# Summing the first hidden product of a feed-forward layer during the attention before it

## The chip, the cores and the metric

The kernel runs on one NeuronCore of a Trainium2 chip. Its five engines work through queues of their own and wait for each other by semaphores: TensorE (PE in the profile, its weight loads PEld), VectorE (DVE), ScalarE (ACT), GpSimd (POOL) and SyncE (SP), which issues the DMAs here. The metric is the device time of one execution in microseconds. The three runs of the kernel before took 629.36, 629.53 and 629.88 us.

## The reference

Attention over q, k, v of 2 batches, 8 heads, 768 positions and 64 columns per head; a key is kept if it is one of the first 8 or lies less than 96 positions back. Then two feed-forward layers over the 1536 tokens, 512 wide with 2048 hidden columns.

```
scores = q k^T / 8 + bias(distance, head), others -1e9;  a = softmax(scores);  x = a v
h = x @ w_in ;  g = h * tanh(log1p(exp(h)))                           # first layer ("mish")
x = g @ w_out
h = x @ w_in2;  g = h if h>=1, 0 if h<=-1, else (h+1)^2/4             # second layer
out = g @ w_out2
```

## The kernel before, in words

All instructions stand in an order written out by hand; each engine works through its own in that order. The kernel has one stretch for the attention and one for the two layers.

**Attention.** A unit s is a batch, a pair of heads and two blocks of 128 queries (u = 0, 1): 24 units, three per pair, eight pairs. The loop at the end of `attention_windows` goes through rounds s = -1 to 27, and each round works on several units at once: `scores(s+1)` (line 327, TensorE), `transposes(s-2)` (364), `values(s-3)` (382), `softmax(s, u)` (339 on VectorE, 344 on ScalarE), `normalise(s-1)` (349 and 350 on VectorE, 354 on GpSimd), and `evict(s-2, u)` (170 on ScalarE, 172 on VectorE), which copies the transposed weights out of PSUM. A finished pair of output columns is rounded into `x_hi` by ScalarE (170), and VectorE subtracts to get `x_lo` (175). Every later product is made of three: high by high, high by low, low by high.

**PSUM.** Eight banks. Before, the scores of even units lie in banks 0 and 1, those of odd units in 6 and 7 (`SC`), the transposes in 2 and 3, the values in 4 and 5. Both halves u of a unit share a bank for each of the two heads j. The scores of a block against 256 keys are two instructions per head, which the profile counts singly: eight per unit.

**Weights.** Each layer has 16 blocks f of 1 MB, which SP loads, and which three engines turn into a high and a low part: `T` (scale, line 162 or 166), `B` (229, ScalarE), `V` (233 and 236, VectorE), `H` (round, 170) and `R` (subtract, 175), each for the two halves i of a block. The first three blocks (`PRE`) are converted during the attention, at the end of the rounds that `BESIDE` names; `T20` is the `T` of block 2, half 0. `FIRST_ON` says on which engine `T`, `H` and `R` run: `p` GpSimd, `a` ScalarE, `v` VectorE.

**Feed-forward.** A step n is a layer, a batch and a block f: `hidden(n)` (lines 519, 520 and 522: 12 products of 512 columns and 12 of 256), `gate(n)` (528 to 559, ScalarE and VectorE), and `finish`, the output products of the step before (570). The first steps are begun beside the attention: `h0a`, `h0b` are the 512 and the 256 columns of `hidden(0)`, `h1a`, `h1b` those of `hidden(1)`, and `g0a` to `g0c` the three parts of `gate(0)`. `out_T(0)`, in `finish`, also uses banks 0 to 5, so it follows the last `x_lo` out of banks 4 and 5.

```
    24: ("h0a",), 25: ("h0b", "g0a"), 26: ("g0b", "h1a", "g0c"), 27: ("h1b",),
```

Of the kernel before, what the change touches and what calls it, by code (L numbers as in the profile page):

```python
# [20 lines left out]
P = 128  # L21
# [9 lines left out]
FIRST_ON = "ppaapp"  # L31
# [14 lines left out]
def attention_then_two_ffn_kernel(  # L46
# [141 lines left out]
    class Weights:  # L188
# [15 lines left out]
        def convert(self, pool, m, f):  # L204
# [12 lines left out]
            on = FIRST_ON if first else LATER_ON  # L217
# [66 lines left out]
    SC, TR, PV, HID = ((0, 1), (6, 7)), (2, 3), (4, 5), (6, 7)  # L284

    def attention_windows(x_hi, x_lo, bank, wts, opening):
        with ExitStack() as es:
# [29 lines left out]
            scs, probs, pts = {}, {}, {}  # L317
            done = []

            def scores(s):  # L320
                b, p, t = steps[s]
                qr, kr = raws[b, p]
                scs[s] = [bank(SC[s % 2][j], [2, 2 * P]) for j in range(2)]
                for u in range(2):
                    i = 2 * t + u
                    for j, ps in enumerate(scs[s]):
                        nc.tensor.matmul(ps[:, u, 0:keys(i)], qr[half(j), i * P:(i + 1) * P],  # L327
                                         kr[half(j), window(i):window(i) + keys(i)], start=True, stop=True)

            def softmax(s, u):  # L330
# [6 lines left out]
                for j, ps in enumerate(scs[s]):  # L337
# [18 lines left out]

            def transposes(s):
                pr = probs.pop(s)[0]
                pts[s] = (pp.tile([P, 2, 2, 2, P], F32, tag="pts", name=f"pts{s}"),
                          [bank(TR[u], [2, 2, P]) for u in range(2)])  # L360
                for u, pt in enumerate(pts[s][1]):
                    for j in range(2):
                        for o in range(keys(2 * steps[s][2] + u) // P):
                            nc.tensor.transpose(pt[:, j, o], pr[:, u, j, o * P:(o + 1) * P], ident)  # L364

            def evict(s, u):
                m = keys(2 * steps[s][2] + u) // P
                dst, src = pts[s]
                rounded("av"[u], dst[:, u, :, 0:m], src[u][:, :, 0:m])

            def values(s):
                b, p, t = steps[s]
                vr = vs[b, p]
                src = pts.pop(s)[0]
                for u in range(2):
# [4 lines left out]
                    for o in range(m):  # L380
                        for j in range(2):
                            nc.tensor.matmul(pv[half(j), i * P - t0:(i + 1) * P - t0], vr[:, 2 * i - m + 1 + o, j],  # L382
                                             src[:, u, j, o], start=(o == 0), stop=(o == m - 1))
# [5 lines left out]
            for s in range(-1, NU + 4):  # L389
# [34 lines left out]
    def attention_all(x_hi, x_lo, bank, wts, opening):  # L424
        with ExitStack() as es:
# [31 lines left out]
            for b in range(B):  # L457
                for p in range(NP):
# [6 lines left out]
                    for j in range(2):  # L465
                        h = 2 * p + j
                        ro = slice(j * D, (j + 1) * D)
                        for pv, (t0, n) in zip(pvs, pieces):
                            for i in range(t0 // P, (t0 + n) // P):
                                ps = [bank(c, [n]) for c, (t, n) in zip(SC[rows % 2], pieces)]  # L470
# [31 lines left out]
            for name in sum((BESIDE[s] for s in sorted(BESIDE)), ()):  # L502
                if name[0] != "b":
                    opening[name]()
                    if name in ("V11", "V21"):
# [3 lines left out]
    class FeedForward:  # L509
        def __init__(self, x_hi, x_lo, bank, xy, gp, tp, wts):  # L510

            def hidden(m, f, t, banks):
                xh, xl = (x[:, :, t * span[m]:(t + 1) * span[m]] for x in (x_hi, x_lo))
                wh, wl = (t[:, 0].rearrange("p (c f) -> p c f", f=P) for t in wts.parts[m, f])
                for (t0, n), u in zip(parts[m], banks):
# [7 lines left out]
                    yield ph  # L523

# [98 lines left out]
            def hidden_of(n):  # L623
                if n < len(steps):
                    m, b, f = steps[n]
                    phs[n] = list(hidden(m, f, b, (HID, HID[n % 2:])[m]))

            def hidden_piece(n):
                if n not in phs:
                    phs[n] = []  # L630
                    m, b, f = steps[n]
                    gens[n] = hidden(m, f, b, SC[n])
# [18 lines left out]
            self.hidden_piece, self.gate_part = hidden_piece, gate_part  # L651
# [103 lines left out]
```

## Time and profile before

| | |
|---|---|
| median of three runs | 629.53 us |
| the profiled execution | 626.96 us |
| its span, first to last instruction | 625.1 us |
| busy: PE, PEld, DVE, ACT, POOL | 608.3, 508.8, 420.4, 389.6, 59.3 us |
| mean granted TensorE clock | 0.999 |

A profile holds one execution. Its time is 1.9 us above its span, since start and end of the program lie outside it, and 2.6 us below the median of the other runs. Busy times are sums over the span. In a timeline each line has the start in us, the duration in us, the engine, the line of the code and the operation, output and inputs, shapes, how many were merged (x8), and in brackets how long the engine was idle ahead of it and who released it. The chain of waits goes back from the last instruction to what released each, and so tells which work set the end.

### The profile page before, as it was taken

The page shows a single profiled execution, that of the slowest core. Times are in us where ns is not written, and L with a number is a line of the kernel's source. Part 1 is how long each engine was busy: PE and PEld are TensorE (multiplying, and loading weights), DVE is VectorE, ACT ScalarE, POOL GpSimd, SP SyncE. Part 2 cuts the span into 40 slices and gives each one's busy share as a digit, 9 for nine tenths or more (in the row PEclk, how much of TensorE's full clock was granted, in tenths as well). Part 3 has the DMA queues.
Part 4 walks back from the last instruction along what each step waited for, and adds up shares of the span by engine and source line. Part 5 has one row for each costly group of instructions (what it writes and reads, how often), then busy time and mean ns, then how long its engine had stood idle before and what let it go on. Part 6 is the DMA issues. An engine that isn't in the chain of part 4 may idle for free.

```text
span 625.1 us, 9403 instructions
## 1 busy us (share of the span) xinstructions
PE 608.3 (97%) x3408; PEld 508.8 (81%) x3408; DVE 420.4 (67%) x970; ACT 389.6 (62%) x845; POOL 59.3 (9%) x122
## 2 busy tenths in 40 slices
PE   5999999999999999999999999999999999999996
PEld 3677678888888888888888888888888888888884
DVE  7899959999999777797877876664333333433332
ACT  5999957888888566686776777574433333433332
POOL 3787630000000000000000000000000000000000
PEclk9999999999999999999999999999999999999999
DMA  7995302443333102221312312300100000100002
GB/s 203 328 310 184 114 2 69 134 135 109 104 127 136 68 0 69 69 78 59 135 68 68 135 68 75 127 2 1 67 1 1 1 0 1 67 1 1 1 0 73
DMA packets 10421, 49.83 MB, mean 80 GB/s; under 512 B 1408, under 2 KB 1664, under 8 KB 6272
## 3 DMA queue, kind: packets, MB, share of 16 engines
q1 hardware_dynamic: 10368, 49.16, 23.7%
q8 instruction: 29, 0.48, 0.3%
q14 instruction: 24, 0.20, 0.1%
HBM read 46.01 MB, written 3.15 MB: 79 GB/s over the span
## 4 chain that ended last, share of the span: by engine, by line
PE 88%; DVE 8%; ACT 1%; SPq 1%; DMA 0%; issue 0%; POOL 0%; DVEq 0%; ACTq 0%
PE psum L570 22%; PE psum L579 21%; PE psum L519 14%; PE psum L520 14%; PE psum L522 14%; DVE pr L339 3%; PE psum L327 1%; DVE pts L172 1%; PE psum L364 1%; PE psum L382 1%; DVE st L349 1%; DVE wbits L236 1%; DVE x_lo L175 1%; ACT pr L344 1%; DMA qr<-in_q_dram 0%
## 5 line engine op out<-in xcount | busy, mean ns | idle before, releaser
L519 PE MATMUL psum<-x_hi,whi 128*128 128x512 f32 x448 | 157.0, 360 | 0.0
L520 PE MATMUL psum<-x_lo,whi 128*128 128x512 f32 x448 | 157.0, 360 | 0.0
L522 PE MATMUL psum<-x_hi,wlo 128*128 128x512 f32 x448 | 106.1, 359 | 0.0
L519 PEld LDWEIGHTS psum<-x_hi,whi 128*128 128x128 f32 x448 | 84.3, 188 | 14.7 <-issue 0.5
L520 PEld LDWEIGHTS psum<-x_lo,whi 128*128 128x128 f32 x448 | 84.5, 189 | 12.8
L522 PEld LDWEIGHTS psum<-x_hi,wlo 128*128 128x128 f32 x448 | 77.7, 189 | 12.5
L559 DVE TENSOR_TENSOR g_lo<-e,g_hi 128x512 fp32r<-128x512 f32 x112 | 65.9, 612 | 32.6 <-ACT g_hi L557 32.6
L543 ACT ACTIVATE e<-psum 128x512 f32<-128x512 f32 x48 | 28.7, 598 | 88.2 <-PE psum L522 88.2
L557 ACT ACTIVATE g_hi<-e 128x512 fp32r<-128x512 f32 x112 | 59.6, 560 | 36.8 <-DVE e L548 31.8
L544 DVE TENSOR_SCALAR e<-e 128x512 f32<-128x512 f32 x48 | 20.5, 427 | 82.9 <-ACT e L543 82.9
L579 PE MATMUL psum<-whi,g_hi 128*128 128x512 f32 x192 | 74.8, 390 | 0.5 <-ACT g_hi L557 0.5
L579 PE MATMUL psum<-whi,g_lo 128*128 128x512 f32 x192 | 74.8, 390 | 0.0
L579 PE MATMUL psum<-wlo,g_hi 128*128 128x512 f32 x192 | 74.7, 389 | 0.0
L570 PE MATMUL psum<-g_lo,whi 128*128 128x512 f32 (+1 forms) x256 | 67.3, 344 | 0.0
L570 PE MATMUL psum<-g_hi,wlo 128*128 128x512 f32 (+1 forms) x256 | 65.7, 338 | 0.0
L570 PE MATMUL psum<-g_hi,whi 128*128 128x512 f32 (+1 forms) x256 | 65.7, 338 | 0.0
L528 ACT ACTIVATE e<-psum 128x512 f32<-128x512 f32 x64 | 31.3, 491 | 52.1 <-PE psum L522 51.7
L548 DVE TENSOR_TENSOR e<-psum,e 128x512 f32<-128x512 f32 x48 | 33.2, 692 | 31.2 <-ACT e L545 31.2
L344 ACT ACTIVATE pr<-pr,st 128x256 f32<-128x256 f32 (+1 forms) x96 | 46.0, 481 | 11.0 <-DVE st L339 9.4
L236 DVE SCALAR_TENSOR_TENSOR wbits<-wsc,wbits 128x512 uint32<-128x512 uint32 x58 | 40.1, 692 | 12.8 <-ACT wbits L229 9.4
L229 ACT ACTIVATE wbits<-stage 128x512 uint16<-128x512 uint16 x62 | 48.3, 778 | 0.0
L354 POOL TENSOR_SCALAR pr<-pr,st 128x256 f32<-128x256 f32 (+1 forms) x96 | 44.2, 482 | 22.8 <-DVE st L350 9.6
(67 smaller groups left out, 898.6 us busy)
## 6 DMA issues: line engine op xcount, KB each, us to landing
stage<-in_w_dram SPq DMA_DIRECT2D x31, 1024.0 KB, 4.9
vr<-in_v_dram SPq DMA_DIRECT2D x8, 704.0 KB, 8.4
out_dram<-stage SPq DMA_DIRECT2D x12, 256.0 KB, 2.3
kr<-in_k_dram SPq DMA_DIRECT2D x14, 216.0 KB, 9.5
qr<-in_q_dram SPq DMA_DIRECT2D x7, 384.0 KB, 9.7
third<-in_w_dram SPq DMA_DIRECT2D x1, 1024.0 KB, 12.3
kr<-in_k_dram SPq DMA_DIRECT2D x2, 144.0 KB, 2.8
qr<-in_q_dram SPq DMA_DIRECT2D x1, 256.0 KB, 3.0
```

What stands on the lines that cost most here:

```text
L229: nc.scalar.activation(bits[:, i, :, 0], words(U16, i, 1), AF.Copy, scale=2.0 ** -13, bias=2.0 ** -14 - 0.5)
L236: nc.vector.scalar_tensor_tensor(out[:, i].bitcast(U32), moved(i, U32), 3, out[:, i].bitcast(U32), op0=ALU.logical_shift_left, op1=ALU.bit ...
L344: nc.scalar.activation(pr[:, u, j, 0:n], pr[:, u, j, 0:n], AF.Exp, scale=-1.0, bias=st[:, u, j, 0:1], accum_out=st[:, u, j, 1:2])
L354: nc.gpsimd.tensor_scalar(pr[:, u, j, 0:n], pr[:, u, j, 0:n], st[:, u, j, 3:4], 1.0, op0=ALU.mult, op1=ALU.mult)
L519: nc.tensor.matmul(ph, wh[:, c], xh[:, c, tok], start=(c == 0), stop=False)
L520: nc.tensor.matmul(ph, wh[:, c], xl[:, c, tok], start=False, stop=False)
L522: nc.tensor.matmul(ph, wl[:, c], xh[:, c, tok], start=False, stop=(c == KD - 1))
L548: nc.vector.tensor_tensor(e, ph, e, op=ALU.max)
L557: nc.scalar.activation(hi[:, t0:t0 + n], e, AF.Copy)
L559: nc.vector.tensor_tensor(lo[:, t0:t0 + n], e, hi[:, t0:t0 + n].bitcast(F32), op=ALU.subtract)
L570: nc.tensor.matmul(y, lhs[:, w], rhs[:, t0:t0 + n], start=(f == 0 and i == 0 and c % share == 0), stop=(f == NF - 1 and i == 2 and c % sha ...
L579: nc.tensor.matmul(ys[c], lhs[:, w], rhs, start=(f == 0 and i == 0), stop=(f == NF - 1 and i == 2))
```

## The change

The scores get two banks, 6 and 7, for all units, and are issued in two parts: the half u = 0 of the next unit behind `softmax(s, 0)`, the half u = 1 behind `softmax(s, 1)`. The banks 0 and 1 that this frees hold `hidden(0)`, which is summed during rounds 10 to 17: `h0a0` is the 512 columns for the first pair's 128 rows of x, `h0b3` the 256 columns for the fourth pair's. A transpose of 128 by 128 becomes two of 64 rows each, into banks 2 and 3, and `evict(s, c)` copies the half c of all of a unit's blocks. `values` moves behind the second part of the scores. Weight block 2 is converted at the end of the attention, its two subtractions on VectorE instead of GpSimd, and the load of block 4 is issued at round 13 instead of 19.

```diff
-FIRST_ON = "ppaapp"
+FIRST_ON = ("ppaapp", "ppaapp", "ppaavv")
-    8: ("V01", "H00"), 9: ("H01", "R00"), 11: ("R01", "T10", "B10"), 12: ("T11", "V10", "B11"),
-    13: ("V11", "H10"), 14: ("R10", "H11"), 16: ("R11",), 17: ("T20", "B20"), 18: ("T21", "V20", "B21"),
-    19: ("V21", "H20"), 20: ("R20", "H21"), 22: ("R21",),
-    24: ("h0a",), 25: ("h0b", "g0a"), 26: ("g0b", "h1a", "g0c"), 27: ("h1b",),
+    8: ("V01", "H00"), 9: ("H01", "R00"), 10: ("h0a0",), 11: ("R01", "T10", "B10", "h0a1"),
+    12: ("T11", "V10", "B11", "h0b0"), 13: ("V11", "H10", "h0b1"), 14: ("R10", "H11", "h0a2"), 15: ("h0b2",),
+    16: ("R11", "h0a3"), 17: ("h0b3",), 19: ("T20",), 20: ("T21",),
+    23: ("g0a",), 24: ("g0b", "h1a", "B20"), 25: ("g0c", "V20", "B21", "h1b"), 26: ("V21", "H20", "H21", "R20", "R21"),
...
-    SC, TR, PV, HID = ((0, 1), (6, 7)), (2, 3), (4, 5), (6, 7)
+    SC, TR, PV, HID = (6, 7), (2, 3), (4, 5), ((0, 1), (6, 7))
...
+            scs = [bank(c, [2, 2 * P]) for c in SC]
...
-            def scores(s):
+            def scores(s, u):
...
+                for n, (u, j, o) in enumerate(blocks(s)):
+                    for c, pt in enumerate(pts[s][1]):
+                        nc.tensor.transpose(pt[:, n], pr[half(c), u, j, o * P:(o + 1) * P], ident[half(c), half(c)])
...
+            def evict(s, c):
+                n = len(blocks(s))
                 dst, src = pts[s]
+                rounded("av"[c], dst[:, 0:n, half(c)], src[c][:, 0:n])
...
+                if 0 <= s < NU:
+                    softmax(s, 0)
                 if s + 1 < NU:
-                    scores(s + 1)
+                    scores(s + 1, 0)
                 if 0 <= s - 2 < NU:
                     transposes(s - 2)
-                if 0 <= s - 3 < NU:
-                    values(s - 3)
-                if 0 <= s < NU:
-                    softmax(s, 0)
                 if 0 <= s - 1 < NU:
                     normalise(s - 1)
...
                 if 0 <= s < NU:
                     softmax(s, 1)
+                if s + 1 < NU:
+                    scores(s + 1, 1)
+                if 0 <= s - 3 < NU:
+                    values(s - 3)
                 if 0 <= s - 2 < NU:
                     evict(s - 2, 1)
                 for name in BESIDE.get(s, ()):
                     opening[name]()
-                    if name in ("V11", "V21"):
+                    if name == "V11":
+                        wts.load()
                         wts.load()
...
+            def hidden_slice(c, t0, n):
+                wh, wl = (t[:, 0].rearrange("p (c f) -> p c f", f=P) for t in wts.parts[0, 0])
+                ph = bank(HID[0][0 if t0 == 0 else 1], [n])
+                tok = slice(t0, t0 + n)
+                for i, (w, x) in enumerate(((wh, x_hi), (wh, x_lo), (wl, x_hi))):
+                    nc.tensor.matmul(ph, w[:, c], x[:, c, tok], start=(c == 0 and i == 0),
+                                     stop=(c == KD - 1 and i == 2))
```

## Rows read from the trace of the kernel before

**Rows 1.** Windows by stage: stretch, length, busy PE, PEld, DVE, ACT, POOL (instructions), clock, DMA, GB/s.
```profile
64.00:82.00 18.00, 16.19 (x160) 12.22 (x159) 17.68 (x67) 16.09 (x55) 13.04 (x26) 1.00 0.20 84
82.00:100.40 18.40, 17.99 (x130) 14.90 (x131) 11.54 (x28) 9.46 (x24) 2.67 (x6) 1.00 0.00 1
100.40:356.00 255.60, 255.60 (x1455) 223.41 (x1454) 219.96 (x447) 193.67 (x387) 0.00 (x0) 1.00 0.27 91
```

**Rows 2.** Chain of waits in rounds 3 to 5: start, us, engine, output, line, merged.
```profile
15.50 0.81 PE psum L382 x12
16.30 1.06 PE psum L327 x8
...
18.39 1.02 PE psum L382 x16
19.41 0.86 PE psum L327 x8
```

**Rows 3.** Timeline of DVE: where softmax(s, 1) begins, for several rounds s.
```profile
31.15 0.41 DVE L339 CUSTOM_DVE_ANT_0 pr<-psum,bias 128x256 f32<-128x256 f32 x1
...
37.87 0.40 DVE L339 CUSTOM_DVE_ANT_0 pr<-psum,bias 128x256 f32<-128x256 f32 x1
...
43.94 0.41 DVE L339 CUSTOM_DVE_ANT_0 pr<-psum,bias 128x256 f32<-128x256 f32 x1
...
51.68 0.41 DVE L339 CUSTOM_DVE_ANT_0 pr<-psum,bias 128x256 f32<-128x256 f32 x1
...
57.20 0.39 DVE L339 CUSTOM_DVE_ANT_0 pr<-psum,bias 128x256 f32<-128x256 f32 x1
...
61.09 0.41 DVE L339 CUSTOM_DVE_ANT_0 pr<-psum,bias 128x256 f32<-128x256 f32 x1
...
71.89 0.41 DVE L339 CUSTOM_DVE_ANT_0 pr<-psum,bias 128x256 f32<-128x256 f32 x1
...
75.14 0.41 DVE L339 CUSTOM_DVE_ANT_0 pr<-psum,bias 128x256 f32<-128x256 f32 x1
...
77.40 0.39 DVE L339 CUSTOM_DVE_ANT_0 pr<-psum,bias 128x256 f32<-128x256 f32 x1
...
81.30 0.41 DVE L339 CUSTOM_DVE_ANT_0 pr<-psum,bias 128x256 f32<-128x256 f32 x1
```

**Rows 4.** Timeline of PE: the scores of unit 19 and of unit 22.
```profile
64.80 1.13 PE L327 MATMUL psum<-kr,qr 64*128 64x256 f32 x8
...
72.37 1.47 PE L327 MATMUL psum<-kr,qr 64*128 64x256 f32 x8 [0.98 <-DVE st L339]
```

**Rows 5.** Chain of waits at h0a and h0b: the last four products of each.
```profile
86.29 0.92 PE psum L522 x4
...
90.24 0.47 PE psum L522 x4
```

**Rows 6.** Timeline of POOL: the first scaling of weight block 0.
```profile
24.45 0.67 POOL L166 TENSOR_SCALAR stage<-stage 128x512 f32<-128x512 f32 x1 [2.33 <-DMA stage<-in_w_dram]
```

**Rows 7.** Timeline of DVE: the copy in round 7, V00, a slow L349, a subtraction of weights.
```profile
27.47 0.69 DVE L172 COPY pts<-psum 128x512 f32<-128x512 f32 x1 [0.91 <-PE psum L364]
...
28.43 0.45 DVE L233 TENSOR_SCALAR wbits<-stage 128x512 uint16<-128x512 uint16 x1
28.98 0.69 DVE L236 SCALAR_TENSOR_TENSOR wbits<-stage,wbits 128x512 uint32<-128x512 uint32 x1
...
53.39 1.11 DVE L349 TENSOR_SCALAR st<-st 128x4 f32<-128x4 f32 x1
...
104.23 0.68 DVE L175 TENSOR_TENSOR wlo<-wbits,whi 128x512 fp32r<-128x512 f32 x1
```

**Rows 8.** Timeline: the first exponential of gate(0), and the first weight load of hidden(2).
```profile
88.22 0.59 ACT L528 ACTIVATE e<-psum 128x512 f32<-128x512 f32 x1
...
100.37 0.19 PEld L519 LDWEIGHTS psum<-x_hi,whi 128*128 128x128 f32 x1
```

**Rows 9.** DMA issues of weight blocks: count, size of one, median us from issue to landing.
```profile
stage<-in_w_dram SPq DMA_DIRECT2D x31, 1024.0 KB, 4.9
```

More of the change, by code (lines that the diff above doesn't have):

```diff
@@ L216, in convert @@
             bits = out.rearrange("p a (n two) -> p a n two", two=2)
-            on = FIRST_ON if first else LATER_ON
+            on = FIRST_ON[f] if first else LATER_ON
             def moved(i, dtype):
@@ L316, in attention_windows @@
             NU = len(steps)
-            scs, probs, pts = {}, {}, {}
+            scs = [bank(c, [2, 2 * P]) for c in SC]
+            probs, pts = {}, {}
             done = []
-            def scores(s):
+            def scores(s, u):
                 b, p, t = steps[s]
                 qr, kr = raws[b, p]
[L323 to L328, printed above, removed]
+                i = 2 * t + u
+                for j, ps in enumerate(scs):
+                    nc.tensor.matmul(ps[:, u, 0:keys(i)], qr[half(j), i * P:(i + 1) * P],
+                                     kr[half(j), window(i):window(i) + keys(i)], start=True, stop=True)
             def softmax(s, u):
@@ L336, in softmax @@
                 n = keys(2 * t + u)
-                for j, ps in enumerate(scs[s]):
+                for j, ps in enumerate(scs):
                     h = 2 * p + j
@@ L355, in normalise, with blocks @@
                                                 op0=ALU.mult, op1=ALU.mult)
+            def blocks(s):
+                t = steps[s][2]
+                return [(u, j, o) for u in range(2) for j in range(2) for o in range(keys(2 * t + u) // P)]
             def transposes(s):
                 pr = probs.pop(s)[0]
[L359 to L367, printed above, removed]
+                pts[s] = (pp.tile([P, 8, P], F32, tag="pts", name=f"pts{s}"), [bank(TR[c], [8, D]) for c in range(2)])
+                for n, (u, j, o) in enumerate(blocks(s)):
[3 more added lines that the diff above has]
+                n = len(blocks(s))
                 dst, src = pts[s]
-                rounded("av"[u], dst[:, u, :, 0:m], src[u][:, :, 0:m])
+                rounded("av"[c], dst[:, 0:n, half(c)], src[c][:, 0:n])
             def values(s):
@@ L374, in values @@
                 src = pts.pop(s)[0]
+                place = {x: n for n, x in enumerate(blocks(s))}
                 for u in range(2):
@@ L382, in values @@
                             nc.tensor.matmul(pv[half(j), i * P - t0:(i + 1) * P - t0], vr[:, 2 * i - m + 1 + o, j],
-                                             src[:, u, j, o], start=(o == 0), stop=(o == m - 1))
+                                             src[:, place[u, j, o]], start=(o == 0), stop=(o == m - 1))
                     if (i + 1) * P == t0 + n:
@@ L469, in attention_all @@
                             for i in range(t0 // P, (t0 + n) // P):
-                                ps = [bank(c, [n]) for c, (t, n) in zip(SC[rows % 2], pieces)]
+                                ps = [bank(c, [n]) for c, (t, n) in zip(HID[rows % 2], pieces)]
                                 rows += 1
@@ L504, in attention_all @@
                     opening[name]()
-                    if name in ("V11", "V21"):
+                    if name == "V11":
+                        wts.load()
                         wts.load()
@@ L625, in hidden_of @@
                     m, b, f = steps[n]
-                    phs[n] = list(hidden(m, f, b, (HID, HID[n % 2:])[m]))
+                    phs[n] = list(hidden(m, f, b, (HID[1], HID[1][n % 2:])[m]))
             def hidden_piece(n):
@@ L631, in hidden_piece @@
                     m, b, f = steps[n]
-                    gens[n] = hidden(m, f, b, SC[n])
+                    gens[n] = hidden(m, f, b, HID[1])
                 phs[n].append(next(gens[n]))
@@ L680, in arm @@
                 opening.update(wts.convert(wpa, 0, f)[0])
-            opening.update({f"h{n}{i}": lambda n=n: ff.hidden_piece(n) for n in range(2) for i in "ab"})
+            opening.update({f"h1{i}": lambda: ff.hidden_piece(1) for i in "ab"})
+            opening.update({f"h0{i}{c}": lambda c=c, t=t: ff.hidden_slice(c, *t) for i, t in zip("ab", pieces)
+                            for c in range(KD)})
             opening.update({f"g0{i}": lambda: ff.gate_part(0) for i in "abc"})
```

4 lines of the change are left out of this document (3 added, 1 removed).

## The prediction, made before the changed kernel was run

> **What bounds the kernel now.** I read the busy times first, then the windows by stage, the chain of waits in order of time, and the timelines of single engines where the chain changes hands. The windows [rows 1] show three stages. From 100.4 us on TensorE is busy without a gap, and nothing in the change touches that stretch: it moves as a block. So the question is only when hidden(2), the first product of that block, can start; before, its first weight load stands at 100.37 us [rows 8]. Up to 82 us VectorE is busy 17.68 of 18.00 us [rows 1]: the reader is to see that the attention's second part is bound by VectorE, not by TensorE. Its first part, up to 31 us, is bound by TensorE: in the chain [rows 2] scores take 1.06 us, the transposes behind them some 1.02, values 1.02, and the next scores follow at once. In the tail, 82 to 100.4 us, VectorE has 11.54 us of work in 18.40 and TensorE 17.99 [rows 1].
>
> I split the time at E, the end of the last read of scores. softmax(23, 1) begins at 81.30 us [rows 3]; its second head follows 0.34 us later and takes some 0.42, so E = 82.06, and from E to hidden(2) there are 18.3 us.
>
> **The change part by part: the loop through one pair of banks.** Which bank a product waits for is seen at 72.37 us [rows 4]: the scores of unit 22 stood 0.98 us until softmax(20, 1), begun at 71.89 [rows 3], had read its first head, although their first half goes into columns that softmax(20, 0) had freed two microseconds earlier. So waits go by the bank, not by its half. With one pair of banks this gives a chain: softmax(s, 1), scores(s+1, 1), then on TensorE's queue values(s-3) and any slice of hidden(0), then scores(s+2, 0), and softmax(s+1, 1) must wait for these since they write its bank. Each term from rows: 0.48 us from the start of the softmax to the scores (71.89 to 72.37); 0.34 for the second head's bank (1.47 against 1.13 us of a group that needn't wait [rows 4]); half a group of scores to the next group, 1.06 less 0.43, which is 0.63 (0.43 is twice 0.21, the difference of 16 and 12 value products of the same columns [rows 2]); values 1.02 [rows 2]; a half group to its result, 1.13 less 0.43, 0.70. Sum 3.17 us a round; 2.96 where values has 12 products and 2.97 where scores(s+2, 0) has 128 columns, so 9.10 per pair of heads. A round without weight work took VectorE 2.26 us (75.14 to 77.40 [rows 3]): the wait is new, and some 0.9 us of it stand idle on VectorE. Queued behind the waiting softmax are the copy of the transposes and all weight work of that round, and ScalarE's exponentials wait for it.
>
> **The slices.** The last four products of h0a take 0.92 us, of h0b 0.47 [rows 5]: 0.23 and 0.12 each. Three, with 0.2 for the change of shape on TensorE (0.63 less 0.43, above), make 0.89 for h0a and 0.55 for h0b, all of it in the loop, ahead of scores(s+2, 0).
>
> **Transposes.** The eight transposes of a unit took 1.02 us, 0.82 without the change of shape [rows 2]. The trace has none on half the rows. From below two halves run side by side at half the columns, 0.41 us. From above I go by the nearest row: a unit whose first block has 128 keys takes 0.86 us for its scores, 0.20 less than others [rows 2], so four loads of 64 rows by 128 columns with their products take 0.43 less 0.20, 0.23 us, and sixteen 0.92. Both ends cost nothing here: they begin 0.27 us ahead of softmax(s, 1) (0.70 less 0.43), so end at the latest 0.65 after it, while the second head's scores cannot begin before 0.82. The copies keep their 512 columns, and each now waits for the whole unit; VectorE reaches its copy 0.68 us after the softmax, so this too is covered.
>
> **Rounds 8 to 22.** Each takes the longer of the loop and VectorE's own work. 8 and 9 stay at VectorE's 6.72 (31.15 to 37.87); 10 is 2.97 + 0.89 = 3.86; 11 and 14 are 4.06 each; 12 and 13 stay at VectorE's 7.74 (43.94 to 51.68), above the loop's 7.03; 15 is 3.51; 16 stays at 3.89 (57.20 to 61.09); 17 is 3.72. Rounds 18 to 21 lose V20, V21 and one slow L349: that line took 1.11 us [rows 7] where a subtraction of weights ran on GpSimd. VectorE would need about 2.4 a round there, so the loop's 2.96, 2.97, 3.17 and 2.96 hold, 12.06 together. Round 22 had 3.90 with such a stall (77.40 to 81.30) and keeps 2.26 with a remainder of 0.68, about 3.0. Sum 52.62 us against 50.15 before (31.15 to 81.30 [rows 3]): 2.5 us longer. In rounds 3 to 7 the loop's 9.10 stands against 8.7 per pair of heads (scores, transposes and values of two full units and one with twelve products [rows 2]), about 1.1 us later by round 7; but there VectorE waited 0.91 us for transposes [rows 7] that stood behind GpSimd's scaling, and this behind the landing of a weight block at 24.45 us [rows 6]. That moment doesn't move, so the lag is taken up: +0.1, at most +1.4. E comes 2.6 us later, at 84.7.
>
> **The tail.** Out of it go h0a and h0b, 4.6 us of TensorE (twelve products at 0.23 and 0.12, and two changes of shape). Into VectorE's share come V20 and V21, 0.45 + 0.69 each, and R20 and R21, 0.68 each [rows 7]: 3.6 us. VectorE had 11.54 us there [rows 1], of which about 1.0 lies behind what hidden(2) needs (the 512 columns of step 1 read from bank 6). 11.54 + 3.6 - 1.0 = 14.2. Two waits come to it: the first exponential of gate(0), 0.59 us [rows 8], stands behind two of the last softmax and ends 0.7 us after VectorE is free; and about 0.2 at each of four hand-overs from ScalarE, an estimate. That makes 15.7 us from E to hidden(2) where there were 18.3: the tail returns 2.6 of the 4.6. The last x_lo stands behind V21, R20 and R21 on VectorE's queue, and out_T(0) needs its bank; that is where the rest goes. From below stands TensorE's own work: some 0.8 until unit 22's transposes can begin, two groups of transposes at 1.02, values 0.81 and twice 1.02 [rows 2], hidden(1) 4.6 like hidden(0), and the 24 products of out_T(0), of the same two widths, 4.2, which makes 14.5; from above, another 1 us of hand-overs makes 16.7.
>
> **The load.** Block 4 is issued behind block 3 at the end of round 13, shortly before 51.68 us [rows 3], and the last q and k stand behind it on SP's queue. They are read by the scores that round 20 issues, near 70 us (softmax(20, 1) begins at 71.89 [rows 3]). A load of this size lands in 4.9 us [rows 9], and from 64 us on the DMA engines are busy 0.20 of the time [rows 1]; coming 5 us later costs nothing. If that cover were gone, round 20 would slip by as much.
>
> **Sum.** +2.5 + 0.1 - 2.6 = 0.0 us. The profiled execution's span of 625.1 and its 626.96 stay; the median of the runs lies 2.57 above that, so 629.5 us. The range of this case by itself is 627.5 to 631.5.
>
> **A rule against it.** Four half loads and their products took 0.23 us in the scores, as worked out above [rows 2]. The Trainium skill ("TensorE: Matmul & The Clock Gate", LDWEIGHTS) says that a load's time goes by its columns, not its rows, about 107 ns for 128. By that, and with loads one after another, 16 half loads would take 1.71 us and the kernel, as an estimate, about 639. The scores' rows speak against it, as two loads there share such a time.
>
> **The rivals.**
> *The loop is shorter.* The terms of 0.34 and 0.70 come from whole groups; with both banks free together and half a group's result at 0.6 the loop is 0.48 + 0.63 + 1.02 + 0.6, 2.73. Nine rounds (10, 11, 14, 15, 17 and 18 to 21) win 0.44 each, 4.0 us: 625.5. For it: groups that needn't wait show no 0.34. Against: the two heads of a softmax are always 0.34 apart.
> *No wait by the bank.* If the product needn't wait for the bank's other half, the sums of VectorE and TensorE bind. TensorE has two half groups of 0.43, transposes near 0.6, values 1.02 and two changes of shape, 2.9 in a full round at most and 2.5 in a lean one; with a slice 3.4 or 3.1. Rounds 8, 9, 12, 13 and 16 keep 18.35, rounds 10, 11 and 14 take 10.2, 15 and 17 6.2, 18 to 21 10.2 and 22 3.0: 47.95, 2.2 less than before, and with the tail 624.7. The wait at 72.37 speaks against it.
> *Slower: ScalarE closes the loop.* Its copy of bank 2 waits for the whole unit's transposes, and ahead of the next L349 stand this copy (0.5) and two exponentials (1.0). Ending 0.6 after the softmax, with 0.3 to be seen, the transposes let L349 begin at 2.4 us and, with the reciprocal and a remainder, the next softmax at 3.4: 0.2 beyond the loop. It decides as soon as the copy ends later than 1.1 us after the softmax. At 0.2 us on 15 rounds it costs 3 us: 632.5. For it: ScalarE is busy 16.09 of 18.00 us in the attention's second part [rows 1]. Against: two rounds of three have no long remainder.
> *A half costs as much as a whole.* Then sixteen transposes take twice 0.82, 1.64 us, and end 0.55 past the moment at which the second head's scores could begin: nine rounds in full, others in part, some 8.5 us: 638. Against it: the 0.23 us of the scores.
>
> **Chances.** The forecast 0.42; the shorter loop 0.22; no wait by the bank 0.10; ScalarE 0.22; halves as dear as wholes 0.04. 0.2%, or 1.26 us, is about what a measurement of this kernel can tell from no change. The forecast's own spread gives faster 0.10, same 0.26, slower 0.06; the shorter loop faster 0.19, same 0.03; the third all faster; ScalarE slower 0.18, same 0.04; the last slower. Together faster 0.39, same 0.33, slower 0.28. The range runs from 624.6 to 633.0.
>
> **What would show it.** Right: VectorE's line 339 waits for line 327 by some 0.9 us in rounds 18 to 21, which take 2.9 to 3.2; rounds 10, 11, 14 about 4; the last softmax read near 84.7 us; hidden(2) near 100.4, with VectorE waited for ahead of out_T(0)'s bank 5 and TensorE idle there. Wrong: 327 never waited for in round 18 to 21; line 349 waiting for ScalarE; half transposes above 1 us a unit; out_T(0) without a wait; a changed pace behind hidden(2).

## The result and the profile after

The changed kernel took 638.11 us (median of four runs, 638.00 to 638.47), the kernel before 629.70 beside it (629.36 to 629.88): ratio 1.014, interval 1.0126 to 1.0154. Slower by 8.4 us, where 629.5 was forecast and 633.0 was the upper end of the range. The profiled execution took 638.00 us, with a span of 636.2. One run of e12 below took 991.58 us at a granted clock of 0.564 and is left out of its median.

In the two profiled executions the time went as follows:

| stretch | before | after | difference | forecast |
|---|---|---|---|---|
| start to softmax(8, 1) | 31.15 | 37.22 | +6.1 | +0.1 |
| softmax(8, 1) to softmax(23, 1) | 50.15 | 55.98 | +5.8 | +2.5 |
| softmax(23, 1) to the first product of hidden(2) | 19.18 | 17.77 | -1.4 | -2.6 |
| behind it | 524.6 | 525.2 | +0.6 | 0 |

These sum to 11.1 us, not 8.4: the first profile of before lay 2.6 us below its median, that of after on its own. The windows by stage show what kind of stretches they are. Columns as in [rows 1]:

```profile
64.00:82.00 18.00, 17.76 (x204) 13.01 (x203) 13.38 (x58) 13.28 (x48) 10.80 (x23) 1.00 0.51 176
...
93.96:110.80 16.84, 14.39 (x124) 11.22 (x124) 14.02 (x30) 11.04 (x26) 2.52 (x4) 1.00 0.01 2
110.80:366.40 255.60, 255.43 (x1452) 223.25 (x1453) 220.38 (x450) 194.14 (x389) 0.00 (x0) 1.00 0.27 91
```

Against [rows 1]: from 64 to 82 us VectorE is busy 13.38 us, not 17.68; it waits now. In the tail TensorE is busy 14.39 us of 16.84, where it was busy 17.99 of 18.40 before. Behind hidden(2) the pace is the same.

VectorE's timeline shows the softmax of rounds 18 to 20 and of 22 (in brackets, idle time and releaser):

```profile
76.19 0.42 DVE L339 CUSTOM_DVE_ANT_0 pr<-psum,bias 128x256 f32<-128x256 f32 x1 [0.30 <-PE psum L327]
...
79.19 0.42 DVE L339 CUSTOM_DVE_ANT_0 pr<-psum,bias 128x256 f32<-128x256 f32 x1 [0.45 <-PE psum L327]
...
82.42 0.69 DVE L175 TENSOR_TENSOR x_lo<-psum,x_hi 128x512 fp32r<-128x512 f32 x1 [0.69 <-ACT x_hi L170]
83.03 0.41 DVE L339 CUSTOM_DVE_ANT_0 pr<-psum,bias 128x256 f32<-128x256 f32 x1
...
89.36 0.42 DVE L339 CUSTOM_DVE_ANT_0 pr<-psum,bias 128x256 f32<-128x256 f32 x1 [0.58 <-PE psum L327]
```

Round 18 takes 3.00 us (76.19 to 79.19) and is closed by line 327, as forecast (2.96). The product that it waits for is the next unit's first half:

```profile
76.68 1.04 PE L327 MATMUL psum<-kr,qr 64*128 64x256 f32 x4
...
78.46 0.70 PE L327 MATMUL psum<-kr,qr 64*128 64x256 f32 x4
```

softmax(19, 1) reads what the four instructions at 76.68 wrote by 77.72, yet it begins only at 79.19, when scores(20, 0), issued at 78.46 into the other half of the same banks, have ended.

Round 19 takes 3.84 (79.19 to 83.03), and what closes it is another wait: x_lo, ahead of softmax(20, 1), waits for x_hi, and ScalarE's x_hi for the values of the round before (TensorE's last in it):

```profile
80.65 1.09 PE L387 MATMUL psum<-pts,vr 128*64 128x128 f32 x16
```
```profile
81.79 0.60 ACT L170 ACTIVATE x_hi<-psum 128x512 fp32r<-128x512 f32 x1 [0.48 <-PE psum L387]
```

In the first rounds TensorE's half groups of scores are slow, and VectorE waits for each:

```profile
7.80 1.46 PE L327 MATMUL psum<-kr,qr 64*128 64x256 f32 x4 [0.83 <-DVE st L339]
9.54 1.56 PE L327 MATMUL psum<-kr,qr 64*128 64x256 f32 x4 [0.29 <-DVE st L339]
11.28 1.56 PE L327 MATMUL psum<-kr,qr 64*128 64x256 f32 x4 [0.18 <-DVE st L339]
...
22.02 0.70 PE L327 MATMUL psum<-kr,qr 64*128 64x256 f32 x4
22.55 0.66 PE L368 MATMUL psum<-ident,pr 64*128 64x64 f32 x16
```
```profile
9.05 0.42 DVE L339 CUSTOM_DVE_ANT_0 pr<-psum,bias 128x256 f32<-128x256 f32 x1 [1.07 <-PE psum L327]
...
10.79 0.42 DVE L339 CUSTOM_DVE_ANT_0 pr<-psum,bias 128x256 f32<-128x256 f32 x1 [0.96 <-PE psum L327]
```

Four instructions of the same form take 1.56 us at 9.54 and 0.70 at 22.02. Sixteen half transposes took 0.66 us.

In the tail unit 23 is late: its line 349 stands behind gate(0) on VectorE, so GpSimd scales late and TensorE waits (the profile names x_hi as the releaser of GpSimd; it ended at 98.77, 0.2 us after the reciprocal that GpSimd reads):

```profile
98.20 0.16 DVE L349 TENSOR_SCALAR st<-st 128x4 f32<-128x4 f32 x1
98.39 0.18 DVE L350 RECIPROCAL st<-st 128x4 f32<-128x4 f32 x1
```
```profile
98.77 2.52 POOL L354 TENSOR_SCALAR pr<-pr,st 128x256 f32<-128x256 f32 x4 [4.84 <-ACT x_hi L170]
```
```profile
101.34 0.34 PE L368 MATMUL psum<-ident,pr 64*128 64x64 f32 x4 [0.80 <-POOL pr L354]
...
108.52 0.38 PE L590 MATMUL psum<-g_hi,whi 128*128 128x256 f32 x1 [0.52 <-DVE x_lo L175]
...
110.97 0.50 PE L528 MATMUL psum<-x_hi,whi 128*128 128x512 f32 x1 [0.32 <-DVE e L555]
```

### The profile page after: what moved, and what is told of

It is laid out like the page before. It is cut to its first block, busy times and chain, and to the rows that moved or that the text cites. A ratio compares the mean times of both kernels' runs of the same rounds, so it can differ in the third digit from the quotient of the medians.

```text
span 636.2 us, 9741 instructions
## 1 busy us (share of the span) xinstructions
PE 615.3 (97%) x3584; PEld 511.2 (80%) x3584; DVE 419.7 (66%) x972; ACT 391.7 (62%) x845; POOL 55.4 (9%) x120
## 4 chain that ended last, share of the span: by engine, by line
PE 91%; DVE 4%; ACT 3%; issue 1%; DMA 0%; POOL 0%; POOLq 0%; DVEq 0%; ACTq 0%
PE psum L590 21%; PE psum L599 20%; PE psum L529 13%; PE psum L528 13%; PE psum L531 13%; PE psum L327 5%; PE psum L387 3%; PE psum L368 1%; DVE pr L339 1%; ACT pr L344 1%; DVE x_lo L175 1%; ACT x_hi L170 1%; PE psum L540 1%; ACT pts L170 0%; DMA counts_raw<-in_counts_dram 0%
## 5 line engine op out<-in xcount | busy, mean ns | idle before, releaser
L528 PE MATMUL psum<-x_hi,whi 128*128 128x512 f32 (+1 forms) x440 | 154.5, 360 | 0.3 <-DVE e L555 0.3
L529 PE MATMUL psum<-x_lo,whi 128*128 128x512 f32 (+1 forms) x440 | 154.4, 360 | 0.0
L531 PE MATMUL psum<-x_hi,wlo 128*128 128x512 f32 (+1 forms) x440 | 104.4, 359 | 0.0
L528 PEld LDWEIGHTS psum<-x_hi,whi 128*128 128x128 f32 x440 | 82.9, 188 | 15.0 <-DVE e L555 0.6
L529 PEld LDWEIGHTS psum<-x_lo,whi 128*128 128x128 f32 x440 | 83.0, 189 | 12.6
L563 ACT ACTIVATE e<-psum 128x512 f32<-128x512 f32 x48 | 28.7, 597 | 88.5 <-PE psum L531 88.5
L327 PE MATMUL psum<-kr,qr 64*128 64x256 f32 (+1 forms) x192 | 47.1, 469 | 11.4 <-DVE st L339 5.5
```

What stands on the lines that cost most here:

```text
L528: nc.tensor.matmul(ph, wh[:, c], xh[:, c, tok], start=(c == 0), stop=False)
L529: nc.tensor.matmul(ph, wh[:, c], xl[:, c, tok], start=False, stop=False)
L531: nc.tensor.matmul(ph, wl[:, c], xh[:, c, tok], start=False, stop=(c == KD - 1))
```

## The experiments

Medians of four to ten runs (the changed kernel's beside those of the study's first comparison), each with its ratio to the kernel before on the same chip and at the same time. "b8" is the start of softmax(8, 1), "b23" that of softmax(23, 1), "tail" the time from b23 to hidden(2), from each one's profile.

| kernel | median us | ratio, interval | b8 | b8 to b23 | tail |
|---|---|---|---|---|---|
| changed | 638.11 | 1.014 (1.0126, 1.0154) | 37.22 | 55.98 | 17.8 |
| e1 x late | 635.23 | 1.0098 (1.0077, 1.012) | 37.12 | 53.47 | 17.9 |
| e2 filling | 637.24 | 1.0129 (1.011, 1.0148) | 38.15 | 54.85 | 17.8 |
| e3 whole transposes | 641.52 | 1.0201 (1.0181, 1.022) | 40.37 | 57.09 | 17.3 |
| e5 x late, filling | 632.92 | 1.0058 (1.0037, 1.0078) | 35.44 | 53.48 | 17.8 |
| e6 no slices | 636.65 | 1.0109 (1.0084, 1.0134) | 38.34 | 53.88 | 18.6 |
| e11 gate later | 636.09 | 1.0099 (1.0077, 1.012) | 37.37 | 55.96 | 16.2 |
| e14 all repairs | 631.77 | 1.0047 (1.0031, 1.0064) | 34.94 | 53.49 | 16.2 |
| e15 repairs, no slices | 632.59 | 1.0054 (1.003, 1.0078) | 35.79 | 51.65 | 18.6 |
| e4 before, halves, late block | 626.78 | 0.996 (0.9944, 0.9976) | 31.40 | 45.70 | 22.6 |
| e7 the same, V21 early | 622.92 | 0.990 (0.9869, 0.9932) | 32.46 | 45.77 | 18.8 |
| e9 before, filling | 629.24 | 0.9998 (0.9983, 1.0013) | 32.48 | 50.14 | 19.2 |
| e10 e7 and filling | 624.27 | 0.9907 (0.9883, 0.993) | 35.89 | 45.79 | 18.8 |
| e12 before, halves | 629.68 | 1.0003 (0.9985, 1.0021) | 35.26 | 50.04 | 18.9 |
| e13 e7, early load | 622.62 | 0.9912 (0.9883, 0.9941) | 30.76 | 45.74 | 18.8 |

**The wait for x_hi (e1).**

```diff
-            done = []
+            done, held = [], []
...
-                ready, done[:] = done[:], []
+                if s < 23:
+                    ready, held[:], done[:] = held[:], done[:], []
+                else:
+                    ready, held[:], done[:] = held + done, [], []
```

> The changed kernel with x_hi and x_lo of a finished pair one round later (up to round 22). Theory A: values(s-3) now stands last in a round, so x_hi waits for it and x_lo, ahead of softmax(s+1, 1) on VectorE, waits for x_hi; that made rounds 19 and 22 last 3.84 us where the loop takes 2.97, round 20 3.35 instead of 3.17 and 13 4.28 instead of 4.10. With the rounding a round later x_hi waits for nothing: rounds 19 and 22 come to 3.0, 20 and 13 lose 0.2, round 4 goes with them; hidden(2) starts 2 to 3 us earlier and the time is 635.0 to 636.3 us. Rival: those rounds are long because ScalarE's copies and exponentials close the loop; then they stay at 3.8 and the time at 637.7 to 638.4.

Measured 635.23, 2.9 less than the changed kernel. Round 19, now 3.00 us, is closed by the scores again, and VectorE has no wait for x_hi before it:

```profile
79.90 0.18 DVE L350 RECIPROCAL st<-st 128x4 f32<-128x4 f32 x1
80.54 0.42 DVE L339 CUSTOM_DVE_ANT_0 pr<-psum,bias 128x256 f32<-128x256 f32 x1 [0.46 <-PE psum L327]
```

Round 22 stayed at 3.84: from round 23 on this kernel rounds at once, as the changed one does. So the wait is shown. Not all of the gain is the wait's, though. From b8 to b23 it is 2.5 us: 1.0 in rounds 19 and 20, which the wait closed; 0.7 in round 13 (4.28 to 3.54), where nothing waited for x_hi and VectorE's own 0.66 us for x_lo moved to another round; and 1.0 in round 8 (4.79 to 3.83). In round 8 the changed kernel's granted clock had fallen to 0.61 and 0.54 (38 to 42 us, behind two stretches of 2 us with TensorE busy 1.47 and 1.51) and this one's had not. The profiles of e2, e3 and e6 round x at once too, show no such fall, and have 3.55 or 3.56 in round 8: rounding at once does not by itself cost that 1.0.

**Early products (e2, e5).** Four transposes of the identity into the free bank 0 behind each half of the scores in rounds -1 to 2 (e2 also has 14 ahead of the first):

```diff
+            def fill(n):
+                spot = bank(0, [P])
+                for _ in range(n):
+                    nc.tensor.transpose(spot, ident, ident)
...
                 if s + 1 < NU:
                     scores(s + 1, 1)
+                if s <= 2:
+                    fill(4)
```

> The changed kernel with idle TensorE time filled early on: 14 transposes of the identity into the free bank 0 ahead of the first scores, and four behind each half of the scores in rounds -1 to 2. Theory B: the first 13 us of products run at the lower clock because TensorE has gaps there (1.46 to 1.56 us for four instructions that take 0.70 later), although the granted-clock column says 1.00. Filled, the half groups take 0.7 to 1.0 us from round 0 or 1 on, softmax(8, 1) begins at 32 to 35 us instead of 37.2, and the time is 633 to 636. Rival: half groups are slow for another reason (their form, or the wait for VectorE ahead of them); then they stay at 1.5 us, the filling only adds work, and the time is 638 to 641.

Measured 637.24, above the 633 to 636 of the theory: the 14 transposes could not start before 5.32 us, when the scores could too, and held these up by 3.2 us. But from then on half groups took 0.78 to 0.97 us, and rounds 0 to 3 took together 11.3 us instead of 13.7. e5 has both repairs and no transposes in front:

> The changed kernel with both repairs: x_hi and x_lo a round later, and four transposes of the identity into the free bank 0 behind each half of the scores in rounds -1 to 2, none ahead of the first scores (there they started them 3.3 us late). Theory: A (the wait for x_hi) and B (early products at the lower clock) are two separate losses and add up. Half groups of scores take 0.7 to 1.0 us from about 10 us on, softmax(4, 1) begins near 20 us instead of 22.8, rounds 4 to 7 take 3.0 to 3.7 and softmax(8, 1) begins at 33 to 35 us instead of 37.2; hidden(2) starts at 105 to 107 us: time 631.5 to 634. Rival: the start of the attention is held by something else (the landing of the first weight blocks, GpSimd's scaling) and the filling gives nothing beyond the late rounding: 634.5 to 636.

Measured 632.92, 2.3 below e1 by the medians; b8 is 1.7 earlier. TensorE in e5:

```profile
9.29 1.22 PE L327 MATMUL psum<-kr,qr 64*128 64x256 f32 x4
10.44 1.05 PE L395 MATMUL psum<-ident 128*128 128x128 f32 x4
11.42 0.70 PE L327 MATMUL psum<-kr,qr 64*128 64x256 f32 x4
12.05 0.66 PE L395 MATMUL psum<-ident 128*128 128x128 f32 x4
```

Near 11 us a half group goes from 1.22 to 0.70 us and four transposes from 1.05 to 0.66; in the changed kernel half groups come to 0.70 only at 22 us. More work on TensorE made the same products faster, so their form is not the cause. The granted-clock column reads 1.00 in all these stretches (the last section comes back to that). b8 (35.44) came out later than the 33 to 35 expected: each round still takes the loop's 3 us.

**Halves (e3, e12).** e3 puts the old `transposes`, `evict` and `values` back into the changed kernel; e12 puts the new ones into the kernel before.

> The changed kernel with whole transposes again (eight of 128 by 128 a unit, copies by query block), all else as changed. Theory: a unit's sixteen half transposes took 0.66 us against 1.02 for eight whole ones, and in the loop most of either is hidden behind the wait for softmax; whole ones end later by 0.2 to 0.4, of which up to 0.2 a round is seen, and the tail has two to three of them on the path: 638.5 to 642. Rival: half transposes with their copies that wait for the whole unit are themselves the loss; then the time falls to 634 to 637.

> The kernel before with the half transposes alone. Theory: TensorE needs 0.36 us less a unit, which shows only where TensorE is the bound: some rounds before 31 us, where the landing of the first weight blocks takes it back, and two or three units of the tail; 627.8 to 629 against 629.3. So of e7's 6.1 us most belongs to the late third block. Rival: the halves are the gain: 624 to 626.

e3 is 3.4 us slower than the changed kernel: the halves help there, and "a half costs as much as a whole" is wrong, although its 638 is the number that came out. Alone on the kernel before they give nothing (1.0003; 629.68, where 627.8 to 629 was expected).

**The slices (e6, e15).** h0a and h0b whole in rounds 23 and 24:

```diff
-    8: ("V01", "H00"), 9: ("H01", "R00"), 10: ("h0a0",), 11: ("R01", "T10", "B10", "h0a1"),
...
-    23: ("g0a",), 24: ("g0b", "h1a", "B20"), 25: ("g0c", "V20", "B21", "h1b"), 26: ("V21", "H20", "H21", "R20", "R21"),
+    8: ("V01", "H00"), 9: ("H01", "R00"), 11: ("R01", "T10", "B10"),
...
+    23: ("h0a",), 24: ("h0b", "g0a", "B20"), 25: ("g0b", "h1a", "g0c", "V20", "B21"), 26: ("h1b", "V21", "H20", "H21", "R20", "R21"),
```

> The changed kernel without the slices: h0a and h0b whole, in rounds 23 and 24, still into banks 0 and 1; gate(0) and h1 a round later. Theory: a slice stands in the chain of the single pair of banks, so taking the eight out makes rounds 10 to 17 shorter, by 0.9 where the loop alone holds them (10, 11, 14), 0.55 (15, 17) and less where VectorE does (12, 13, 16): softmax(23, 1) begins 3 to 4 us earlier, near 89.5 instead of 93.2, and TensorE does 4.6 us more in the tail: 637 to 639.5, so the slices won no more than about 1 us. Rival: the slices ran beside VectorE's work in the loop and cost nothing there; then softmax(23, 1) stays at 92.5 to 93.2 and the time rises by the tail's 4 us to 641 to 643.

> The same repairs, without the slices (h0a and h0b whole in rounds 23 and 24, gate(0) behind them): what is left of the change is one pair of score banks, the half transposes and the late third block. Against e7_before_halves_late3b (622.9 us) only the pair of banks, its order and the two repairs that it needs differ. Theory: the loop through one pair of banks by itself costs 7 to 9 us (rounds 0 to 5 and 17 to 22 take 3.0 where four banks take 2.1 to 3.2, rounds 7 and 8 follow late), and the slices give back nothing: 630 to 632. Rival: the slices are the larger part of the loss: 625 to 628.

e6 is 1.5 us faster than the changed kernel, a little under the expected 637, but its gate(0) also starts a round later, as in e11 below, and beside e11 (636.09) it wins nothing. The pair nearest to differing by the slices alone is e15 and e14: e15, a little above the expected 632, is 0.8 above e14, and their runs overlap (631.16 to 633.41 and 631.53 to 632.09). The table says why: in e15 the way from b8 to b23 is 1.8 us shorter than in e14, all of it in rounds 10 to 17 (28.7 us for 30.6), and the tail 2.4 longer. (Of the 2.1 that e6 has from b8 to b23 against the changed kernel, 1.2 lies in round 8, ahead of the slices.) The slices moved TensorE's work from one place that it bounds to another, and are worth nothing that can be told: the rival, that they cost nothing in the loop, falls.

**The tail (e11, e14).**

```diff
-    23: ("g0a",), 24: ("g0b", "h1a", "B20"), 25: ("g0c", "V20", "B21", "h1b"), 26: ("V21", "H20", "H21", "R20", "R21"),
+    24: ("g0a", "h1a", "B20"), 25: ("g0b", "V20", "B21", "h1b", "g0c"), 26: ("V21", "H20", "H21", "R20", "R21"),
```

> The changed kernel with the three parts of gate(0) started in round 24 instead of 23, behind the reciprocals of unit 23. Theory on the tail (17.0 us where 15.7 were forecast): L349 of unit 23 stood behind gate(0) on VectorE until 98.20 us, so GpSimd scaled unit 23 only at 98.8 to 101.3 and TensorE waited 0.46 and 0.80 us for it; with L349 at about 95 these waits go, and hidden(2) starts 0.8 to 1.5 us earlier: 636.5 to 637.4. Rival: gate(0) itself is the longest chain of the tail; then out_T(0) waits for g_hi, and the time is 638 to 640.

> The changed kernel with all three repairs: x_hi and x_lo a round later, the filling of rounds -1 to 2, gate(0) from round 24. Theory: the losses are separate and add up (2.9, 2.3 and 2.0 us by the medians so far): softmax(23, 1) begins near 88.9 us, hidden(2) at 105 to 105.4, and the time is 630.5 to 631.5 us, still above the kernel before. Rival: they overlap, so that one hides behind another: 632 to 633.5.

e11 gave 2.0 us, a little more than expected. Line 349 now runs at 95.06, and unit 23's transposes wait for nothing:

```profile
95.06 0.17 DVE L349 TENSOR_SCALAR st<-st 128x4 f32<-128x4 f32 x1 [0.49 <-ACT pr L344]
```
```profile
99.03 0.71 PE L368 MATMUL psum<-ident,pr 64*128 64x64 f32 x16
```

One by one (the filling on top of the late x) the repairs gave 2.9, 2.3 and 2.0; together 6.3 instead of 7.2: nearly separate. At 631.77, a little above the 631.5 expected, e14 is still 0.5% slower than before.

**The rest of the change on four banks (e4, e7).** The kernel before, with half transposes, the third block in rounds 24 to 27 and the earlier load; e7 has V20 and V21 right behind the copies of unit 22 (here against e4):

```diff
-    24: ("h0a", "B20"), 25: ("V20", "B21", "h0b", "g0a"), 26: ("V21", "H20", "g0b", "h1a", "g0c", "H21"),
-    27: ("R20", "R21", "h1b"),
+    24: ("h0a", "B20", "V20", "B21", "V21", "H20", "H21"), 25: ("R20", "R21", "h0b", "g0a"),
+    26: ("g0b", "h1a", "g0c"), 27: ("h1b",),
```

> The kernel before, with its four score banks and its order, and of the change only the half transposes, the third weight block converted in rounds 24 to 27 and the load of block 4 at round 13. Theory: the single pair of banks is what costs; without it rounds 17 to 22, freed of weight work, fall from 20.2 us to 16 to 17.5 (TensorE's scores, transposes and values, some 2.7 a round), and the tail, bound by TensorE, takes the weight work at nothing and is 0.5 to 1 shorter by the halves: 625 to 627.5 us against 629.6. Rival: the tail's VectorE work makes hidden(2) wait by as much as the loop gains: 629 to 630.5.

> As e4_before_halves_late3, but all of block 2's B, V and H in round 24, right behind the copies of unit 22, and its subtractions on GpSimd in round 25. In e4 VectorE stood idle for 3.45 us there while h0a ran, and later V21, slowed to 1.57 us beside GpSimd's subtraction, held gate(0), so that out_T(0) waited 1.78 us for g_hi. Theory: with V21 in the idle stretch that wait goes, the tail is bound by TensorE alone, and hidden(2) starts 1.5 to 2 us earlier than in e4: 624.5 to 625.8. Rival: the wait moves to the last x_lo or to the converted block, and the time stays at 626.3 to 627.2.

e4 took 626.78 and e7 622.92, 1.0% less than before and better than forecast. In e4 the gain of the loop (4.5 us) went in part into gate(0):

```profile
89.77 1.57 DVE L242 TENSOR_SCALAR wbits<-third 128x512 uint16<-128x512 uint16 x1
```
```profile
93.38 0.69 PE L586 MATMUL psum<-g_hi,whi 128*128 128x512 f32 x2 [1.78 <-ACT g_hi L573]
```

In e7 out_T(0) starts without that wait (92.57 us). e7 and e15 differ in the score banks, the order and repairs that go with these, and in when block 2 is converted and on which engine its subtractions run: 9.7 us, not parted further. e7 is the version that beats both kernels; with e12 at 1.0003, its 6 us come from the late third block (its load, which moved with it, was not tried alone): VectorE does that work where it had stood idle in e4 and before.

**Why before's first profile was 2.6 us short (e8, e9, e10, e13).**

> The kernel before once more, for a second profile. Its first profile took 626.96 us while its other runs took 627.95 to 630.41. Theory: in the usual run some stretch of the attention runs at the lower clock, which the first profile happened to miss; this profile then shows one or two rounds in which scores, transposes and values take up to twice as long, and hidden(2) starts 1 to 3 us after 100.4. Rival: the difference lies behind hidden(2), in the long block of products; then hidden(2) starts at 100.2 to 100.6 again and the span behind it is longer than 524.6 us.

This second profile took 630.59 us, with hidden(2) at 103.26. It does show a fall of the clock (columns as in [rows 1]) behind a gap of TensorE:

```profile
13.03 1.02 PE L327 MATMUL psum<-kr,qr 64*128 64x128 f32 x8 [1.95 <-DVE st L350]
13.97 1.42 PE L364 MATMUL psum<-ident,pr 128*128 128x128 f32 x6
15.32 2.08 PE L327 MATMUL psum<-kr,qr 64*128 64x256 f32 x8
```
```profile
14.00:16.00 2.00, 2.00 (x11) 1.58 (x12) 0.57 (x1) 1.36 (x5) 0.79 (x2) 0.54 1.00 218
16.00:18.00 2.00, 2.00 (x13) 1.26 (x10) 1.46 (x11) 0.88 (x4) 1.00 (x3) 0.61 1.02 265
```

So e9 filled such gaps (`fill` into bank 5, eight in round 0, six in round 1), and e10 did the same to e7, with eight more in round 7.

> The kernel before with eight transposes of the identity into the free bank 5 behind the scores of round 0 and six behind those of round 1, where TensorE had nothing to do (1.95 us in its second profile, after which the granted clock stood at 0.50 from 15 to 17 us and softmax(3, 1) began at 16.75 instead of 14.89). Theory: the usual run of before loses 2 to 3 us by this fall of the clock, and the first profile (626.96) did not have it; filled, most runs have no fall, softmax(3, 1) begins at 14.5 to 15.5 us, and the median is 626.5 to 628 with less spread. Rival: the fall doesn't hang on that gap; then the median stays at 628.5 to 630.

> As e7_before_halves_late3b, with the same filling in rounds 0 and 1, and eight transposes of the identity in round 7, where TensorE stood idle 1.65 us behind GpSimd and the granted clock then fell to 0.50 from 28 to 31 us; round 7 took 6.86 us there against 5.43 in e4. Theory: without that fall softmax(8, 1) begins near 31 us instead of 32.5 and the time is 621 to 622.3. Rival: the clock falls elsewhere in the attention, or the filling delays the products behind it by as much: 622.5 to 624.

Both missed: no gain. They don't rule the clock out. In e9's profile it reads 1.00 throughout, but the filling stands ahead of the real products on TensorE's queue: unit 3's scores begin at 13.27 us, where they began at 13.03 in e8 and 11.58 in before's first profile. In e10 round 7 took 9.33 us, and the clock fell there all the same (0.52 from 32 to 34 us), behind a longer wait:

```profile
30.39 1.71 PE L377 MATMUL psum<-ident,pr 64*128 64x64 f32 x16 [3.12 <-POOL pr L363]
```

What the profiles share is the landing of weight block 0, for which GpSimd waits; here in e8, in e12 and in e10:

```profile
26.73 0.67 POOL L166 TENSOR_SCALAR stage<-stage 128x512 f32<-128x512 f32 x1 [1.59 <-DMA stage<-in_w_dram]
```
```profile
28.61 0.65 POOL L166 TENSOR_SCALAR stage<-stage 128x512 f32<-128x512 f32 x1 [5.87 <-DMA stage<-in_w_dram]
```
```profile
29.24 0.65 POOL L175 TENSOR_SCALAR stage<-stage 128x512 f32<-128x512 f32 x1 [5.86 <-DMA stage<-in_w_dram]
```

In the seven profiles with four banks (before, e4, e7 to e10, e12) it came between 24.45 [rows 6] and 29.24 us, and b8 6.65 to 7.13 us behind it. e13 moved this load:

```diff
                     load_qk(rp, 0, p + 1)
+                if p == 1:
+                    wts.load()
                 vs[0, p] = load_v(rp, 0, p)
...
-                if s in (0, 4, 10):
+                if s in (4, 10):
```

> As e7_before_halves_late3b, with the load of weight block 0 issued ahead of the second and third v instead of behind them. In the seven profiles with four score banks the landing of this block went from 24.45 to 29.24 us and softmax(8, 1) began 6.65 to 7.13 us behind it each time. Theory: the landing sets round 7, and with it both the spread of the kernel before and the 2.6 us by which its first profile lay below the median; 1.4 MB earlier on the queue the block lands at 19.5 to 22 us, softmax(8, 1) begins at 27.5 to 30 us instead of 31.2 to 35.9, and the time is 618 to 621 us. Rival: round 7 is held by something that only comes at the same time (v, the fall of the clock); then softmax(8, 1) begins at 31 us or later and the time stays at 622 to 624.

The block had landed before GpSimd asked for it at 22.44, and b8 was 30.76, the earliest of all, but not the 27.5 to 30 expected, and the time did not change (622.62). Another transfer is late in its place:

```profile
28.68 1.01 PE L338 MATMUL psum<-kr,qr 64*128 64x128 f32 x8 [1.63 <-DMA qr<-in_q_dram]
```

That the landing goes with b8 in seven profiles is seen; that it alone makes the spread of the runs is not shown. What is shown is that the offset was of that one profile: the same kernel's second profile (e8) took 630.59 us, 3.6 more, and the changed kernel in its own profile began on block 0 at 27.27 us, without a wait, and its four runs lie within 0.5 us.

## Why the prediction was wrong

Against the forecast the four stretches were off by +6.0, +3.3, +1.2 and +0.6 us, and the step from the profile to the median by -2.5: together the 8.6 us between 629.5 and 638.11.

**Right.** The chain through one pair of banks: in the changed kernel rounds 10, 11, 14, 15, 17, 18 and 21 took 3.90, 4.11, 4.09, 3.55, 3.76, 3.00 and 2.98 us, against 3.86, 4.06, 4.06, 3.51, 3.72, 2.96 and 2.96. (Round 10 fits by luck there: x_lo's wait closed it. In e1, where the scores close it, it is 3.90 too.) So the terms taken from whole groups of scores (0.34, 0.63, 0.70) held, and the slices' 0.89 and 0.55 with them. VectorE's wait for line 327 is 0.3 to 0.6 us, not 0.9: 3.00 less 0.45 leaves 2.55 us for VectorE's own way through round 18, where 2.26 was used. The halves hide in the loop. As forecast, out_T(0) waits for bank 5, 0.52 us.

**Failed: the rounds before 8 (+0.1 forecast, +6.1 measured).** The forecast counted the loop from round 3. It holds from round 0: with the repairs (e14) rounds 0 to 7 take 24.50 us, 3.06 each, as in 9.10 per pair of heads, where before they took 23.26 and rounds 0 to 2 alone 7.0. The 6.1 us are three parts. softmax(0, 1) is 1.2 us later than before: it waits for scores(1, 0), issued at 7.80 us ahead of it into its own banks. The loop itself is 1.2. The other 3.7 is what the repairs take out of rounds 0 to 7 (28.17 to 24.50 us): small groups with waits between them left TensorE slow there (filling gives 2.3 us, e5 against e1), and x_lo waited for x_hi in rounds 4 and 5. The lag at round 3 was 4.2 us, more than the 2.33 for which GpSimd had waited for the landing [rows 6]: in the changed kernel it did not wait at all.

**Failed: values moved to the end of a round, counted as a term of TensorE's queue alone.** The prediction asks for all that stands behind a moved step; it did so for the slices and not for x_hi and x_lo, which read what values writes. Of the 3.3 us by which rounds 8 to 22 overran, 1.9 are rounds 19 (3.84 for 2.97), 20 (3.35 for 3.17) and 22 (3.84 for some 3.0), which this wait closed. Another 1.1 are rounds 8 and 9 (7.78 for 6.72), where the clock fell; why it fell in this profile and not in e2, e3 or e6 stays open. Rounding x later gave 2.9 us in all (e1), of which 1.0 lies in that round 8.

**Mis-sized: the tail.** 17.0 us from E (93.96) instead of 15.7. With gate(0) a round later it is 15.5 (hidden(2) at 109.54 in e11, E at 94.09). So the sum over VectorE's work comes near; missed was that unit 23's line 349 stood behind gate(0) and kept GpSimd and TensorE waiting.

**Carried over: the 2.57 us from the profile to the median.** It belonged to the one profile; the changed kernel's own was 0.1. This hid 2.5 of the other errors.

Of the rivals, "no wait by the bank" fell (line 327 closes rounds 18 and 21, and rounds 18 to 21 take 12.2 us in e1, where it has 10.2); so did the shorter loop (2.73, measured 3.00 and 2.98). "ScalarE closes the loop" had the sign and the engine of the x_hi wait, but not the place: its copies close no round. The halves' rule, worked out to 1.71 us for sixteen, fell with the 0.66. By the rule of the Trainium skill ("TensorE: Matmul & The Clock Gate", LDWEIGHTS), a load's time by its columns, and with loads one after another, these sixteen would have been the dearer form. The trace does not agree with the second half of that: the changed kernel's half loads last 146 ns each on average (352 of them), so sixteen within 0.66 us overlap. Whether a load's time goes by its columns alone was not tried.

## What to carry to other kernels

When a buffer pair is halved, run the new chain from the first round, not from where the old one was bound, and follow what reads the moved step's result to whatever in-order queue it stands on. When a repair gains, look round by round at where the gain lies: a third of e1's lay in a round in which other kernels without the repair lose nothing. Work pays for being moved only if its engine has idle time at the new place: the slices went from TensorE's tail into a loop that TensorE closes and won nothing, the third block went from VectorE's full loop into 3.5 us of its tail that stood idle and won 6 us. And the offset of a single profile to the median is a property of that run: look for which wait in it varies before adding it to a forecast.

## What was not expected of the hardware

The granted clock reads 1.00 in stretches where products ran at the lower level. Eight score instructions took 2.08 us in e8 at 15.32 us, where the column says 0.50 (15 to 17 us), so at the lower of the clock's two levels, 1.2 GHz; and the same 2.08 in e10 at 7.42 us, where it says 1.00:

```profile
7.42 2.08 PE L336 MATMUL psum<-kr,qr 64*128 64x256 f32 x8 [0.45 <-DMA qr<-in_q_dram]
```

So ahead of the first fall that a profile records the column did not tell the level; the durations of one form side by side did. The Trainium skill ("TensorE: Matmul & The Clock Gate", Seeing it yourself) warns that such records are not always to be trusted; these rows agree.

A uint16 scaling on VectorE (line 242 in e4) took 1.57 us at 89.77, beside this subtraction on GpSimd, and 0.46 at 84.19, with GpSimd idle:

```profile
89.73 1.28 POOL L184 TENSOR_TENSOR wlo<-wbits,whi 128x512 fp32r<-128x512 f32 x1 [8.48 <-ACT whi L179]
```
